# Attention and two dense layers on one core: the four transfers of q of items 8 to 15 issued by ScalarE instead of SyncE

## The chip, the cores and the metric

One Trainium2 chip, one of its cores. The time of a kernel is the device time of one execution in microseconds (us), the median of the runs shown. A profile is one further execution, recorded by the hardware profiler. Engines are called as in the profile: PE is TensorE, PEld its weight loads, DVE is VectorE, ACT is ScalarE, POOL is GpSimd, SP is SyncE, which computes nothing and issues transfers. An engine's name with a q (SPq, ACTq) is its instruction queue: there stand the instructions that issue transfers or wait.

## What is computed

Three steps follow each other. Attention takes q, k and v of shape (4 batches, 8 heads, 576 positions, 64). Then come two dense layers over the 2304 x 512 result: a maximum of three products followed by an output product, and a product of two products followed by an output product.

```python
q_d, k_d, v_d = (x.reshape(B, H, S // 4, 4, D).mean(axis=3) for x in (q, k, v))
out_up = np.repeat(sm_attn(q_d, k_d, v_d), 4, axis=2)
scores = np.where(np.abs(pos[:, None] - pos[None, :]) < 4, scale * q @ k.T, -1e9)
out_local = softmax(scores) @ v
x = (out_up + out_local).transpose(0, 2, 1, 3).reshape(2304, 512)
h = np.maximum(np.maximum(x @ w1, x @ w2), x @ w3) @ w_out
return ((h @ w_a) * (h @ w_b)) @ moe2_w_out
```

## The kernel before, in words

**Items.** The attention is cut into 16 items, each two heads of one batch. An item goes through these steps: k and q are loaded (`a_load_qk`), v is loaded in two forms (`a_load_v`: vr for the averaged attention, L248, and vw for the local windows, L272), k and q are turned so that the head dimension lies on partitions (`a_qk`), scores and softmax (`a_scores`: exponentials on ACT at L376 and L395, normalisations on POOL at L401 and L408), transposes of the probabilities (`a_tr`: POOL folds four rows of v together at L419 and L420, PE transposes, ACT copies out of PSUM at L435 and L447) and the products with v (`a_av`, L456 and L478, sums on DVE at L488, high and low parts on ACT at L501 and POOL at L502).

**Two ways to turn k and q.** Items 0 to 7 are loaded with rows of 64 numbers and turned by PE (L309, L314). Items 8 to 15 (`i >= TV`) are loaded so that each 32 x 32 block already stands in place: four transfers for k and four for q (L228), each 32 partitions x 576 numbers, 72 KB in pieces of 32 numbers. DVE then turns the blocks (L296 for k, L297 for q).

**Buffers.** The tiles of k, q, vr and vw have one buffer in each pool. Items 8 to 15 alternate between the pools `ap_` (even) and `ex2` (odd); items 0 to 7 alternate between `ap_` (even) and `ex` (odd). So the load of an item waits until the item two before it has been read in the same pool: q for L297 of that item, vr for L420 of that item. The first tile in `ex2` (item 9) has no such wait.

**Order of the work.** Up to the line `ctx.enter_context(tc.manual_schedule())` (L1422) the program's tile framework decides the order of each engine's instructions. It plays the program through a timeline of its own with the priorities that the code gives (the strings LOOP and LOOPS set in which order the steps of different items are written: k is the load of k and q, v the load of v, Q the turning, S, T and A the rest). Work of the first dense layer is mixed in as filler (`dense`, matmuls at L700), and pieces of its weights are loaded at L523 and converted on DVE, ACT and POOL (L544 to L567). An engine then runs its own list strictly in order; an instruction that waits holds everything behind it on that engine. From L1422 on the order is written out by hand, and the change touches nothing there.

**What the change touches.** Line L228 alone. In the kernel before, all transfers of the attention are issued by SP.

Of the kernel before, what the change touches and what calls it, by code (L numbers as in the profile page):

```python
# [64 lines left out]
def attn_moe_kernel(  # L65
# [14 lines left out]
    nc = tc.nc  # L80
# [121 lines left out]
    def pool2(i):  # L202

        return ex2 if i >= NI // 2 and i % 2 else pool(i, 2)
# [12 lines left out]
    def a_load_qk(i):  # L217
        b, hp = items[i]
        s = st[i]
        h = 2 * hp  # L220
        engs = (nc.sync, nc.scalar if i < ACT_LOADS else nc.sync)
        if i >= TV:
            for nm, src in (("k", k), ("q", q)):
                x = pool2(i).tile([P, (RF + 1) * 2 * D], F32, tag=nm, bufs=1, name=nm)
                s[nm] = x[:, :S]
                for j in range(P // BS):
                    hh, d0 = divmod(j * BS, D)
                    nc.sync.dma_start(  # L228
                        x[j * BS : (j + 1) * BS, :S].rearrange("p (c d) -> p c d", d=BS),
                        src[b, h + hh, :, d0 : d0 + BS].rearrange("(c p) d -> p c d", p=BS),  # L230
                    )
            return
        for eng, nm, src in zip(engs, "kq", (k, q)):
            s[nm] = pool2(i).tile([P, RF + 1, 2, D], F32, tag=nm, bufs=1, name=nm)
            for j in range(2):
                eng.dma_start(
                    s[nm][:, :RF, j, :], src[b, h + j, : RF * P].rearrange("(r p) d -> p r d", p=P)
                )
            eng.dma_start(
                s[nm][:RT, RF], src[b, h : h + 2, RF * P :].rearrange("h p d -> p h d")  # L240
            )
# [1146 lines left out]
    def emit(f, i):  # L1388
        if i < NI and (f, i) not in emitted:
            emitted.add((f, i))  # L1390
            {"k": a_load_qk, "v": a_load_v, "Q": a_qk, "S": a_scores, "T": a_tr, "A": a_av}[f](i)
# [283 lines left out]
```

## Time and profile before

| | |
|---|---|
| median of 3 runs | 848.06 us (846.41 to 849.1) |
| the profiled execution's own time | 848.16 us |
| its span, first to last instruction | 846.4 us |
| mean granted TensorE clock | 0.982 |
| PE busy | 818.0 us (97%) |
| DVE, ACT, POOL busy | 650.9, 355.6, 441.0 us |
| attention's transfers of lines L228, L248, L272 | from 57.6 us on for L228, until 182 us for L272 |

The chain that ended last is the path of work, followed back from the last instruction. A timeline row gives start, duration, engine, line, operation, output and inputs, the number of merged instructions, and in brackets how long the engine had been idle before and what ended the wait.

### The profile page before, as it was taken

The page shows a single profiled execution, that of the slowest core. Times are in us where ns is not written, and L with a number is a line of the kernel's source. Part 1 is how long each engine was busy: PE and PEld are TensorE (multiplying, and loading weights), DVE is VectorE, ACT ScalarE, POOL GpSimd, SP SyncE. Part 2 cuts the span into 40 slices and gives each one's busy share as a digit, 9 for nine tenths or more (in the row PEclk, how much of TensorE's full clock was granted, in tenths as well). Part 3 has the DMA queues.
Part 4 walks back from the last instruction along what each step waited for, and adds up shares of the span by engine and source line. Part 5 has one row for each costly group of instructions (what it writes and reads, how often), then busy time and mean ns, then how long its engine had stood idle before and what let it go on. Part 6 is the DMA issues. An engine that isn't in the chain of part 4 may idle for free.

```text
span 846.4 us, 15417 instructions
## 1 busy us (share of the span) xinstructions
PE 818.0 (97%) x5785; PEld 767.2 (91%) x5785; DVE 650.9 (77%) x1220; ACT 355.6 (42%) x812; POOL 441.0 (52%) x417
## 2 busy tenths in 40 slices
PE   5988799999999999999999999999999999999998
PEld 3767589999999999999989999999999999999997
DVE  4896986754989688689689689798888745577775
ACT  4785555544343223324246543444443432333331
POOL 3876586535456335546557645545554543355541
PEclk9699989999999999999999999999999999999999
DMA  7899975200321111320144554454442358766612
GB/s 175 182 191 163 171 124 110 43 21 2 124 75 50 51 50 50 137 75 26 68 156 174 189 189 168 179 187 171 178 174 106 143 207 330 259 225 224 225 51 74
DMA packets 125555, 116.33 MB, mean 137 GB/s; under 512 B 81834, under 2 KB 108202, under 8 KB 125482
## 3 DMA queue, kind: packets, MB, share of 16 engines
q1 hardware_dynamic: 121162, 98.06, 39.9%
q10 hardware_dynamic: 4320, 17.30, 5.7%
q8 instruction: 45, 0.74, 0.4%
q14 instruction: 28, 0.23, 0.1%
HBM read 80.74 MB, written 34.60 MB: 136 GB/s over the span
## 4 chain that ended last, share of the span: by engine, by line
PE 86%; DMA 5%; DVE 3%; POOL 3%; issue 1%; SPq 1%; ACT 1%; POOLq 0%; DVEq 0%; ACTq 0%
PE ps_m L700 40%; PE ps_u L1091 30%; PE ps_q L865 5%; PE ps_m L1241 4%; DMA vr<-in_v_dram 2%; PE ps_av L478 1%; PE ps_tl L441 1%; DMA raw<-in_moe_w_out_dram 1%; PE ps_ud L456 1%; PE ps_s L358 1%; PE ps_sd L340 1%; PE ps_m L865 1%; DMA vw<-in_v_dram 1%; POOL vr L419 1%; PE ps_td L430 1%
## 5 line engine op out<-in xcount | busy, mean ns | idle before, releaser
L700 PE MATMUL ps_m<-xh,w 128*128 128x384 f32 x864 | 173.7, 339 | 0.3 <-ACT xh L501 0.3
L700 PEld LDWEIGHTS ps_m<-xh,w 128*128 128x128 f32 x864 | 151.2, 189 | 1.7 <-ACT xh L501 0.6
L1091 PE MATMUL ps_u<-xh,w 128*128 128x384 f32 x720 | 136.8, 336 | 0.1
L1091 PEld LDWEIGHTS ps_u<-xh,w 128*128 128x128 f32 x720 | 125.3, 188 | 1.9 <-DVE acc L756 0.5
L1091 PE MATMUL ps_u<-xl,w 128*128 128x384 f32 x648 | 122.5, 335 | 0.4 <-ACT sn L1103 0.4
L1091 PEld LDWEIGHTS ps_u<-xl,w 128*128 128x128 f32 x648 | 112.9, 188 | 2.2 <-ACT sn L1103 0.7
L1103 ACT COPY sn<-ps_u 128x384 f32<-128x384 f32 x108 | 51.2, 479 | 123.5 <-PE ps_u L1091 120.3
L1281 POOL TENSOR_TENSOR gl<-g,gh 128x384 fp32r<-128x384 f32 x52 | 54.7, 1053 | 83.3 <-ACT gh L1280 83.3
L700 PE MATMUL ps_m<-xl,w 128*128 128x384 f32 x432 | 94.4, 337 | 0.2 <-POOL xl L502 0.2
L700 PE MATMUL ps_m<-wo,gh 128*128 128x512 f32 (+1 forms) x316 | 92.4, 390 | 0.0
L700 PEld LDWEIGHTS ps_m<-xl,w 128*128 128x128 f32 x432 | 76.5, 188 | 0.9 <-POOL xl L502 0.4
L700 PEld LDWEIGHTS ps_m<-wo,gh 128*128 128x128 f32 x316 | 58.4, 188 | 9.6
L729 DVE TENSOR_TENSOR t<-ps_m,t 128x384 f32<-128x384 f32 x48 | 26.4, 551 | 45.1 <-PE ps_m L700 38.4
L1022 POOL TENSOR_TENSOR w<-F,w 128x768 fp32r<-128x768 f32 (+1 forms) x36 | 56.3, 1578 | 9.2 <-ACT w L1020 8.7
L551 ACT ACTIVATE ce<-ce,ebias 128x512 int16<-128x512 uint16 x60 | 43.4, 723 | 41.0 <-DVE ce L544 41.0
L1350 DVE TENSOR_TENSOR acc<-ps_m,acc 128x512 f32<-128x512 f32 (+1 forms) x67 | 45.0, 677 | 18.7 <-PE ps_m L700 18.4
L554 DVE SCALAR_TENSOR_TENSOR ce<-raw,ce 128x512 uint16<-128x512 uint16 x60 | 49.8, 830 | 3.6 <-ACT ce L551 3.5
L1115 DVE TENSOR_TENSOR ca<-ps_u,sn 128x384 f32<-128x384 f32 x54 | 30.0, 555 | 28.8 <-PE ps_u L1091 17.9
L1033 POOL TENSOR_TENSOR F<-F 128x256 f32<-128x256 f32 x24 | 20.1, 839 | 59.3 <-DVE F L561 49.5
L700 PE MATMUL ps_m<-wo,gl 128*128 128x512 f32 (+1 forms) x158 | 48.9, 391 | 0.0
L1233 DVE TENSOR_TENSOR acc<-ps_m,acc 128x512 f32<-128x512 f32 (+1 forms) x62 | 33.3, 552 | 15.4 <-PE ps_m L1241 13.1
L544 DVE TENSOR_SCALAR ce<-raw 128x512 uint16<-128x512 uint16 x60 | 39.1, 652 | 2.1 <-DMA raw<-in_moe_w_dram 1.7
(209 smaller groups left out, 1684.6 us busy)
## 6 DMA issues: line engine op xcount, KB each, us to landing
dw<-w SPq DMA_DIRECT2D x24, 768.0 KB
raw<-in_moe_w_dram SPq DMA_DIRECT2D x18, 512.0 KB
raw<-in_moe_w_out_dram SPq DMA_DIRECT2D x18, 512.0 KB
w<-dw SPq DMA_DIRECT2D x12, 768.0 KB
w<-dw ACTq DMA_DIRECT2D x12, 768.0 KB
dw<-wo SPq DMA_DIRECT2D x12, 512.0 KB
vw<-in_v_dram SPq DMA_DIRECT2D x62, 80.0 KB
vr<-in_v_dram SPq DMA_DIRECT2D x16, 288.0 KB
```

The lines of the kernel that those rows point to most:

```text
L544: nc.vector.tensor_scalar(out=e, in0=top, scalar1=0x7FF0, scalar2=None, op0=ALU.bitwise_and)
L551: nc.scalar.activation(out=s16, in_=e, func=AF.Relu, bias=ebias, scale=8.0)
L554: nc.vector.scalar_tensor_tensor(out=e, in0=top, scalar=0x8000, in1=e, op0=ALU.bitwise_and, op1=ALU.bitwise_or)
L700: nc.tensor.matmul(ps, lhs[a], rhs[b], start=(i == 0), stop=(i == n - 1))
L865: nc.tensor.matmul(ps, sw[c0, n][a][:, m * P : (m + 1) * P], hq[n][b], start=start and k == 0, stop=k == 2, skip_group_check=not start,)
L1022: nc.gpsimd.tensor_tensor(out=l, in0=w, in1=h.bitcast(F32), op=ALU.subtract)
L1091: nc.tensor.matmul(ps, w[:, a, slot, kk], y[:, b * HK + kk], start=start and i == 0, stop=i == 3 * HK - 1, skip_group_check=not start,)
L1103: nc.scalar.copy(t, ps)
L1233: nc.vector.tensor_tensor(out=a, in0=x, in1=a, op=ALU.add)
L1241: nc.tensor.matmul(y, lhs[a], tw[c, n][b], start=start and k == 0 and t == ts.start, stop=k == 2, skip_group_check=True,)
L1281: nc.gpsimd.tensor_tensor(out=l, in0=g, in1=h.bitcast(F32), op=ALU.subtract)
L1350: nc.vector.tensor_tensor(out=a, in0=ps, in1=a, op=ALU.add)
```

## The change

The four transfers of q of an item from 8 to 15 are issued from ACT's queue. Those of k stay on SP's. Nothing else is edited.

```diff
@@ -225,7 +225,7 @@
                 s[nm] = x[:, :S]
                 for j in range(P // BS):
                     hh, d0 = divmod(j * BS, D)
-                    nc.sync.dma_start(
+                    (nc.scalar if nm == "q" else nc.sync).dma_start(
                         x[j * BS : (j + 1) * BS, :S].rearrange("p (c d) -> p c d", d=BS),
                         src[b, h + hh, :, d0 : d0 + BS].rearrange("(c p) d -> p c d", p=BS),
                     )
```

## Rows read from the trace of the kernel before

**Rows 1.** The page's first part: busy time, share and instructions of each engine

```profile
PE 818.0 (97%) x5785; PEld 767.2 (91%) x5785; DVE 650.9 (77%) x1220; ACT 355.6 (42%) x812; POOL 441.0 (52%) x417
```

**Rows 2.** Busy time by stretch: stretch, us, engines busy, PEclk, DMA share, GB/s

```profile
57.00:70.00 13.00, 12.52 (x206) 9.96 (x208) 11.55 (x35) 9.95 (x31) 9.13 (x12) 1.00 0.94 164
70.00:80.00 10.00, 8.85 (x122) 7.08 (x114) 5.96 (x14) 6.37 (x20) 5.66 (x8) 1.00 0.91 160
80.00:90.00 10.00, 5.18 (x95) 3.95 (x95) 8.82 (x19) 1.90 (x5) 6.24 (x7) 0.95 0.94 161
90.00:100.00 10.00, 9.67 (x130) 7.83 (x127) 9.06 (x21) 6.38 (x20) 7.00 (x7) 0.88 0.93 166
100.00:110.00 10.00, 7.43 (x36) 6.07 (x36) 10.00 (x23) 5.79 (x19) 7.24 (x8) 0.80 1.13 190
110.00:120.00 10.00, 10.00 (x127) 8.37 (x126) 7.80 (x22) 6.84 (x22) 8.25 (x10) 0.86 0.56 117
120.00:130.00 10.00, 10.00 (x100) 9.61 (x99) 7.48 (x21) 4.50 (x12) 7.61 (x9) 1.00 0.73 119
```

**Rows 3.** The chain that ended last, 0 to 110 us: start, us, what

```profile
63.74 4.29 DMA vr<-in_v_dram
...
70.78 5.13 DMA vr<-in_v_dram
...
98.81 3.82 DMA vr<-in_v_dram
```

**Rows 4.** Timeline of SP: the transfers as it issues them

```profile
67.37 3.31 SPq L228 DMA_DIRECT2D q<-in_q_dram  x6
70.78 1.67 SPq L248 DMA_DIRECT2D vr<-in_v_dram  x2
...
95.26 2.06 SPq L228 DMA_DIRECT2D q<-in_q_dram  x4
...
98.81 0.42 SPq L248 DMA_DIRECT2D vr<-in_v_dram  x1
...
132.65 0.31 SPq L248 DMA_DIRECT2D vr<-in_v_dram  x1
```

**Rows 5.** Timeline of POOL

```profile
62.71 0.72 POOL L420 TENSOR_TENSOR vd<-vr 72x256 f32<-72x256 f32 x1
...
76.04 1.27 POOL L419 TENSOR_TENSOR vr<-vr 72x512 f32<-72x512 f32 x1 [3.72 <-DMA vr<-in_v_dram]
...
95.82 0.72 POOL L420 TENSOR_TENSOR vd<-vr 72x256 f32<-72x256 f32 x1
...
102.76 1.86 POOL L419 TENSOR_TENSOR vr<-vr 72x512 f32<-72x512 f32 x1 [3.97 <-DMA vr<-in_v_dram]
...
136.74 1.29 POOL L419 TENSOR_TENSOR vr<-vr 72x512 f32<-72x512 f32 x1 [1.73 <-DMA vr<-in_v_dram]
```

**Rows 6.** Timeline of DVE

```profile
71.66 0.78 DVE L297 STREAM_TRANSPOSE qt<-q 128x576 f32<-128x576 f32 x1 [2.21 <-DMA q<-in_q_dram]
...
81.18 1.11 DVE L547 TENSOR_SCALAR cm<-raw 128x512 uint32<-128x512 uint32 x1 [3.56 <-POOL w L567]
```

**Rows 7.** Timeline of PE

```profile
88.81 0.30 PE L345 MATMUL ps_s<-cap,identb 128*128 128x320 bf16 x1 [3.50 <-DVE el L392]
...
106.04 1.33 PE L441 MATMUL ps_tl<-ident,el 128*128 128x128 f32 x5 [2.45 <-POOL el L408]
```

**Rows 8.** Lines L228 and L1077: engine, operation, count, ns min/median/max, first and last start

```profile
L228 SPq DMA_DIRECT2D q<-in_q_dram x32: 384/496/764, 60.3 to 139.9; - x32
...
L1077 ACTq DMA_DIRECT2D w<-dw x18: 326/326/443, 690.8 to 797.0; - x18
L1077 ACTq DMA_DIRECT2D raw<-dw x6: 326/486/1466, 695.0 to 790.4; - x6
```

**Rows 9.** Timeline of ACT

```profile
73.05 0.63 ACT L566 CAST w<-cm 128x512 fp32r<-128x512 f32 x1 [3.12 <-DVE cm L561]
```

**Rows 10.** Waits of SP's queue, 57 to 120 us: total us, times, longest

```profile
SPq L228 <- DVE sd L398: 1.0, 1, 1.0
```

## Prediction

> **What bounds the kernel now.** I read the page first: PE is busy for 97% of the span [rows 1]. So a change in the attention counts only where PE stands still or runs slowly, and the next view to read is the busy time by stretch. From 120 us on PE has no gap: 10.00 of 10 us at a granted clock of 1.00. The stretch in which the moved transfers start is another matter. From 57 to 120 us PE is busy for 12.52 + 8.85 + 5.18 + 9.67 + 7.43 + 10.00 = 53.65 of 63 us, so it idles for 9.35 us; and from 80 to 120 us its granted clock is 0.95, 0.88, 0.80 and 0.86, which withholds 0.5 + 1.2 + 2.0 + 1.4 = 5.1 us of full-rate time [rows 2]. These 14.5 us are all that can be won. No time saved later than 120 us can count.
>
> The third view is the chain that ended last, as far as 110 us. Transfers of vr stand on it three times, of 4.29, 5.13 and 3.82 us [rows 3]. They are not slow: one issued at 132.65 us, where SP has little to do, releases POOL's addition at 136.74 us, 4.09 us later [rows 4, 5]. They start late. The timeline of SP shows why: ahead of the vr at 70.78 us stand six transfers of q that take 3.31 us to issue, and ahead of the one at 98.81 us four of q, 2.06 us [rows 4]. Their buffers had long been free. The first (item 7) reuses the buffer of item 5, read by the sixth L420, which ends at 62.71 + 0.72 = 63.43 us. The second (item 10) reuses that of item 8, read by the ninth, which ends at 95.82 + 0.72 = 96.54 us [rows 5]. So SP's strict order made these transfers wait for 7.35 and 2.27 us.
>
> What follows from it is in the timelines of POOL, DVE and PE. POOL idles 3.72 us before its addition at 76.04 us and 3.97 us before the one at 102.76 us [rows 5]. Behind the first stands a weight conversion on POOL that DVE awaits for 3.56 us, until 81.18 us; DVE also lost 2.21 us at 71.66 us to q itself [rows 6]. PE pays a little later, 3.50 us before 88.81 us and 2.45 us before 106.04 us [rows 7]. In each case the low clock follows the gap [rows 2].
>
> **The change, part by part.** It removes 32 issues from SP, each with a median of 496 ns, between 60.3 and 139.9 us [rows 8]: 15.9 us of SP's time. Eight of them, those of items 8 and 9, fall before 71 us.
>
> Gain 1, the vr of item 7: without the six q issues it starts 3.3 us earlier. POOL's wait of 3.72 us nearly goes, and DVE's 3.56 us with it. DVE has other work up to then and is busy for 8.82, 9.06 and 10.00 of 10 us afterwards [rows 2], so it is the next to be late. I take 3.0 us; the bounds are 0 (DVE or ACT late instead) and 3.56.
>
> Gain 2, the vr of item 10: it can start at 96.6 instead of 98.81 us, 2.2 us earlier, and POOL's wait falls from 3.97 to about 1.8 us. PE's gap of 2.45 us stands behind that addition by way of POOL's L408, so I take 2.0 us, with bounds of 0 and 2.2.
>
> Gain 3, the clock: the two gaps of PE come before the low-clock stretches. If both shrink below what lowers the clock, up to 5.1 us return; if neither does, nothing. I take 1.0, because gap 1 keeps part of its cause, DVE's load.
>
> The cost is on ACT. The nearest rows for an issue from ACT are 326 ns for a 768 KB transfer and 486 ns for another (longest 1466) [rows 8]; the same pieces cost SP 496 ns, and I take that value. It makes 2.0 us per item and 15.9 us in all, bounded by 32 x 0.326 = 10.4 us and, with one slow issue per item, 8 x (3 x 0.496 + 1.466) = 23.6 us. From 70 to 130 us ACT idles for 60 - 31.8 = 28.2 us [rows 2], against 24 x 0.496 = 11.9 us: covered, if the issues stand in those gaps. An example is the 3.12 us that ACT waits before 73.05 us [rows 9]. From 57 to 70 us it is not covered: ACT idles there for 13 - 9.95 = 3.05 us against 8 x 0.496 = 4.0 us. Behind the issues stand the copies out of PSUM and the exponentials, and PE and DVE wait for these. The earlier q repays part of it, because DVE's wait of 2.21 us [rows 6] becomes shorter. I take a net cost of 2.0 us; the bounds are 0 and 4.0 plus the waits below.
>
> A wait is also moved. From item 10 on a q issue waits until DVE has turned the q two items before it (L297). On SP the longest wait of this line is 1.0 us, once [rows 10]. On ACT such a wait would hold L376, L395, L435 and L447 of older items. Lower bound 0, upper bound 1.0 us for each of the 6 items from 10 on, 6 us; I take 0, as the one long wait is alone among 64 issues. SP's remaining issues only move forward, and no instruction on POOL or DVE is added. After 120 us eight or so of the issues fall where PE has no gap, and I price them at nothing. What hides them is ACT's idle time, 5.5 of 10 us [rows 2]; without it each item would cost up to 2.0 us.
>
> The sum, against the profiled execution (848.16 us, span 846.4, so 1.8 us around it): -3.0 - 2.0 - 1.0 + 2.0 = -4.0, and 848.16 - 4.0 = 844.2. That execution is 0.1 us above the median of 848.06, so 844.1 us against the median.
>
> **The first rival: ACT becomes what SP was; slower.** Place: ACT from 57 to about 110 us, where q's issues stand in front of copies that PE needs. Price: 2.0 us for each of the five items 8 to 12 that are loaded while PE has no reserve, 10 us. The gains are then halved by the late ACT, -2.5, and the clock falls no less often. Result: 848.1 + 7.5 = 855.6 us at worst and about 852 if half of it is covered. It decides when two or more items are issued while ACT has other work ready, or ahead of L297 of the item that frees the buffer. For it speaks ACT's 9.95 of 13 us up to 70 us; against it the 28.2 us of idle time after that [rows 2]. The order on ACT is written by the planner's own timeline, and the trace of before cannot show it; that raises the chance. I give this 0.32.
>
> **The second rival: the transfers themselves are the limit; no change.** The 16 DMA engines are 0.94, 0.91, 0.94 and 0.93 busy from 57 to 100 us [rows 2], and q's share is unchanged by the edit: the same pieces of 128 bytes. A vr issued earlier would share the engines with q and land no earlier: 848.1 us. Against it: vr takes 4.29 and 3.82 us in the crowd [rows 3] and 4.09 us out of it [rows 4, 5], so no queue stands in front of it; and the share reaches 1.13 in one stretch, so 0.93 is not the ceiling [rows 2]. The Trainium skill (DMA: Bandwidth & Descriptors, Issuing engines are not separate DMA queues) speaks against the change here: transfers from SP and ACT run on the same 16 engines and interleave, and a second issuer saves the sequencer's time alone, which it calls usually small relative to the transfer. By that rule the result would be 848.1 us. The trace agrees that the engines are shared, but not that the issue time is small here: six issues take 3.31 us next to a vr of 4 to 5 us [rows 3, 4]. Together with the case in which gains and costs cancel (gains of 3, costs of 3) I give no change 0.20.
>
> **A third: more moves than the diff says.** The planner orders the whole attention anew once q has another queue. Filler and conversions can change places by some us either way. I can price that only as a widening of both sides by 2 us; a better or worse order counts in the chances above.
>
> **How the numbers follow.** Forecast, faster: 0.48; no change 0.20; slower 0.32. The measurement of this kernel can tell about 0.3% from no change, 2.5 us. The forecast's own range reaches from 838.5 (gains 3.56 + 2.2, most of the clock, a cost of 1 us) to 845.5 us. For 8 in 10 the range must take in no change and the half-covered rival: 839.5 to 853.0, which leaves out the worst of the first rival and the best of the forecast.
>
> **What the profile of the changed kernel would show.** SP: 32 q issues fewer, and item 7's vr issued near 67 us. POOL: the waits for vr of 3.72 and 3.97 us shorter by about 3 and 2 us. DVE: no wait of 3.56 us behind POOL's conversion and none of 2.2 us for q. PE: less than 6 us idle from 57 to 120 us. ACT: 32 issues of about 0.5 us. The forecast is wrong if PE's or DVE's waits for ACT (L315, L435, L447, L395) grow by more than 4 us in all, if ACT stands before q issues for L297, or if vr takes 6 us or more from issue to landing while q is under way from ACT.

## The result, and the profile after

The changed kernel is slower: 854.38 us, the median of 4 runs (853.26 to 854.98), against 847.93 us for the kernel before in the same sitting (846.41 to 849.1). The ratio is 1.0073, with a 95% interval of 1.0056 to 1.0091. That is 6.45 us, more than the 0.3% that a measurement can tell, and 1.4 us above the range of the prediction.

The first part of the page of after answers to [rows 1].

```profile
PE 819.0 (96%) x5785; PEld 768.4 (90%) x5785; DVE 656.6 (77%) x1220; ACT 354.7 (42%) x812; POOL 441.1 (52%) x417
```

PE does the same work in a span of 853.2 us, 6.8 us longer. ACT's computing takes 354.7 us; it was 355.6. The 32 transfers that it issues now aren't in this number, because the profile doesn't count issues as busy time.

**Where the time goes** is read from busy time by stretch: from, to, us, then the busy time of PE, PEld, DVE, ACT and POOL with their instructions, the granted clock, the DMA share and GB/s. First the kernel before, for the two longer stretches that [rows 2] don't have:

```profile
0.00:57.00 57.00, 43.17 (x498) 32.74 (x498) 43.30 (x108) 35.15 (x110) 34.91 (x53) 0.82 0.87 184
57.00:120.00 63.00, 53.66 (x691) 43.27 (x691) 53.19 (x131) 37.24 (x114) 43.52 (x49) 0.92 0.91 160
```

Then the kernel after:

```profile
0.00:57.00 57.00, 37.92 (x436) 29.20 (x437) 39.58 (x97) 32.28 (x101) 31.43 (x50) 0.82 0.92 176
57.00:120.00 63.00, 53.70 (x699) 43.18 (x697) 55.77 (x132) 36.37 (x110) 41.27 (x45) 0.92 1.00 158
...
57.00:70.00 13.00, 9.74 (x118) 7.48 (x117) 6.60 (x23) 4.82 (x14) 5.66 (x7) 0.74 1.20 169
...
120.00:150.00 30.00, 29.33 (x354) 26.04 (x350) 23.35 (x54) 15.49 (x45) 21.82 (x25) 1.00 0.68 117
```

PE loses 43.17 - 37.92 = 5.25 us in the first 57 us, in which the kernel before issued none of the moved transfers. From 57 to 120 us, the stretch that the prediction was made of, nothing changes on balance: 53.70 and 53.66 us at the same clock. After 120 us PE now has 0.67 us of gaps. These make 5.9 of the 6.8 us.

A second reading confirms that the loss lies early. L488 is the sum that ends an item's attention; two stand per item. The row of the line gives count, ns, and the first and last start: before, then after.

```profile
L488 DVE TENSOR_TENSOR x<-ps_av,up x32: 407/445/464, 32.2 to 201.0; 128x290 f32<-128x290 f32 x16, 128x286 f32<-128x286 f32 x16
```

```profile
L488 DVE TENSOR_TENSOR x<-ps_av,up x32: 409/444/460, 37.1 to 207.9; 128x290 f32<-128x290 f32 x16, 128x286 f32<-128x286 f32 x16
```

The first sum comes 4.9 us later and the last 6.9 us. Behind the last, 846.4 - 201.0 = 645.4 us were left before and 853.2 - 207.9 = 645.3 us are left after. In the traces of all variants below this rest is 644.9 to 645.6 us. So one number, the start of the last L488, tells of any variant what it cost.

**What else the trace of after shows.** The transfers of L228: on which queue, count, ns min/median/max, first and last start.

```profile
L228 ACTq DMA_DIRECT2D q<-in_q_dram x32: 317/332/668, 0.7 to 148.0; - x32
L228 SPq DMA_DIRECT2D k<-in_k_dram x32: 311/402/1472, 34.5 to 148.5; - x32
L228 ACTq EVENT_SEMAPHORE  x10: 17/28/5022, 56.3 to 144.8; - x10
```

The first q no longer starts at 60.3 us [rows 8] but at 0.7 us. Item 9's tile is the first in its pool and waits for no buffer, so the planner made its four issues the first instructions of ACT. The timelines of ACT and PE show what this does to the first turn (in after; in before PE began the turn of k at 4.38 us and that of q at 6.13 us):

```profile
0.74 2.18 ACTq L228 DMA_DIRECT2D q<-in_q_dram  x4
...
4.99 1.09 PE L309 MATMUL ps_t<-ident,k 128*128 128x128 f32 x4 [4.99 <-DMA k<-in_k_dram]
7.54 1.11 PE L309 MATMUL ps_t<-ident,q 128*128 128x128 f32 x4 [1.47 <-DMA q<-in_q_dram]
```

Later, ACT stands at the first issue of item 8. Timelines of ACT and of DVE in after:

```profile
56.57 0.22 ACT L316 COPY kt<-ps_t 128x64 f32<-128x64 f32 x1
61.55 1.87 ACTq L228 DMA_DIRECT2D q<-in_q_dram  x2
63.53 0.47 ACT L395 ACTIVATE el<-el 128x320 f32<-128x320 f32 x1 [6.74 <-DMA q<-in_q_dram]
...
64.03 0.49 DVE L405 TENSOR_REDUCE eps<-el 128x5 f32<-128x320 f32 x1 [4.45 <-ACT el L395]
```

ACT computes nothing for 6.74 us, its queue waits for 5.02 us at one instruction, and DVE then waits 4.45 us for ACT. The issue does not wait for L297. The kernel's instruction list tells for what: the transfers of SP and ACT take eight completion semaphores in turn, and a transfer waits until the one that had its semaphore before has landed. For ACT's first issue of item 8 the list reads

```
L228 DMA q<-in_q_dram 32x18x32 [waits DMAHW5,DMAHW4,DMAHW6,DMAHW3,DMAHW7,DMAHW1,DMAHW0]
```

that is, for landings on seven of the eight, all of transfers that SP issued. Six of them are earlier loads of q. The seventh, DMAHW4, is the semaphore that this issue takes itself: the transfer that had it before is the first load of k of item 7, which SP issued only at 56.16 us.

Last, the planner wrote another order of the whole attention, for all engines. SP's own loads moved too: in after, SP issues two transfers of k of item 9 ahead of those of k of item 5.

```profile
34.52 0.95 SPq L228 DMA_DIRECT2D k<-in_k_dram  x2
35.58 2.81 SPq L236 DMA_DIRECT2D k<-in_k_dram  x2
```

In before, the first transfer of L228 starts at 57.58 us. So three theories stood: **A**, item 9's early transfers and the new order of the first 57 us; **B**, ACT's time (the first rival); **C**, ACT's waits for landings of SP's transfers.

### The profile page after: what moved, and what is told of

Same layout as the page of the kernel before. It is cut to its first block, busy times and chain, and to the rows that moved or that the text cites. A ratio compares the mean times of both kernels' runs of the same rounds, so it can differ in the third digit from the quotient of the medians.

```text
span 853.2 us, 15403 instructions
## 1 busy us (share of the span) xinstructions
PE 819.0 (96%) x5785; PEld 768.4 (90%) x5785; DVE 656.6 (77%) x1220; ACT 354.7 (42%) x812; POOL 441.1 (52%) x417
## 4 chain that ended last, share of the span: by engine, by line
PE 81%; DMA 7%; DVE 5%; POOL 3%; issue 2%; SPq 1%; ACT 1%; POOLq 0%; DVEq 0%; ACTq 0%
PE ps_m L700 37%; PE ps_u L1091 30%; PE ps_q L865 4%; PE ps_m L1241 4%; DMA vr<-in_v_dram 4%; DMA q<-in_q_dram 1%; DMA raw<-in_moe_w_out_dram 1%; PE ps_m L865 1%; POOL xl L502 1%; PE ps_s L358 1%; PE ps_av L478 1%; PE ps_sd L340 1%; DMA k<-in_k_dram 1%; PE ps_ud L456 1%; POOL el L408 1%
## 5 line engine op out<-in xcount | busy, mean ns | idle before, releaser
L544 DVE TENSOR_SCALAR ce<-raw 128x512 uint16<-128x512 uint16 x60 | 42.9, 716 | 4.5 <-DMA raw<-in_moe_w_out_dram 3.9
```

The costliest lines, as they stand in the source:

```text
L544: nc.vector.tensor_scalar(out=e, in0=top, scalar1=0x7FF0, scalar2=None, op0=ALU.bitwise_and)
```

## The experiments

The ratios are to the kernel before, measured in the same sitting. Executions of the kernel before ranged from 844.48 to 851.44 us in one sitting (29 runs), so verdicts rest on the ratios, and a trace is read only for where a wait stands.

### Which items' transfers carry the loss

Each of these replaces the condition at L228 and leaves the planner free.

```diff
-(nc.scalar if nm == "q" else nc.sync).dma_start(
+(nc.scalar if nm == "q" and i == 9 else nc.sync).dma_start(    # e1
+(nc.scalar if nm == "q" and i == 8 else nc.sync).dma_start(    # e2
+(nc.scalar if nm == "q" and i != 9 else nc.sync).dma_start(    # e3, e9
```

Item 9 alone (e1). 

> Only the four q transfers of item 9 go to ACT; all others stay on SP. Theory A (the early issue): nothing holds item 9's q back, so the planner puts it first on ACT, the first loads of items 0 and 1 come later and the order of the first 57 us is another; most of the loss is there. It expects 851 to 854 us against 848, PE's first turn of q near 7.5 us instead of 6.1, and PE busy for some 38 of the first 57 us as in the changed kernel. Theory B (ACT's time: 2 us per item that is moved, the first rival): one item of eight, so 0.9 us at most, 848 to 849 us. Theory C (ACT waits for landings of SP's transfers, worst at item 8): no loss here, 848 us.

Measured: 855.62 us, ratio 1.0087 (1.0057 to 1.0117), above even A's range. Four issues in place of 32 give the whole loss, and the last of them starts at 2.4 us, so ACT spends no time on q later. B falls.

Item 8 alone (e2). 

> Only the four q transfers of item 8 go to ACT. Theory C: ACT stands about 5 us near 56 us, before the first of them, until transfers that SP issued have landed, and this costs 2 to 5 us: 850 to 853 us. Theory A: no early issue, 848 us, give or take what the new order costs. Theory B: 0.9 us at most, 848 to 849 us.

Measured: 848.17 us, 1.0005 (0.9987 to 1.0024): no difference. ACT's longest wait for a landing is 1.7 us here, so this is no test of C.

All but item 9 (e3). 

> As the changed kernel, but item 9's q stays on SP: seven items on ACT. Theory A: the loss at the start is undone, PE's first turn of q is back near 6.1 us and the time is 847 to 850 us. Theory B: seven eighths of the loss remain, 853 to 854 us. Theory C: ACT's wait of about 5 us near 56 us remains, 850 to 853 us.

Measured: 844.67 us, 0.9961 (0.9945 to 0.9977). It beats both kernels, which no theory had expected, although ACT stands 4.5 us at item 8's issue.

### Taking the early issue away

The `with` lines are cut behind the condition: what follows is the issue, from ACT for all q in e4 and for item 9's q in e6 and e7.

```diff
+with tc.issue_after(mark["q", i - 2].ins) if nm == "q" else ExitStack():                # e4
+with tc.issue_after(mark["q", 0].ins) if nm == "q" and i == 9 else ExitStack():         # e6
+with tc.issue_after(mark["q", 7].ins) if nm == "q" and i == 9 else ExitStack():         # e7
+(nc.scalar if nm == "q" and i >= 10 else nc.sync).dma_start(                            # e5
+(nc.scalar if i >= 10 else nc.sync).dma_start(                                          # e8, k and q
```

All q on ACT, each held behind L283 of the item two before (e4). 

> As the changed kernel, but the planner is told to queue each item's q transfers on ACT behind the scaling of q of the item two before (the L283 that follows the turn that frees the buffer). No early issue, and ACT's order up to 57 us is that of the kernel before. Theory A: the loss at the start is gone, 845 to 849 us, and the gains on POOL's waits for vr may show. Theory B: all eight items still cost ACT their 2 us, 853 to 855 us. Theory C: the 5 us wait near 56 us shrinks to under 2 us because the issue stands later, but waits of 1 to 2 us at other items remain, 848 to 852 us.

Measured: 854.26 us, 1.0082 (1.0059 to 1.0105). A's expectation missed: without an early issue the kernel is as slow. C's missed too: ACT stands 6.8 us at one issue, not under 2.

Items 10 to 15 (e5). 

> Items 10 to 15 issue q from ACT, items 8 and 9 from SP. If ACT's stand of 3 to 6 us before item 8's first issue is a cost (it waits there for landings of transfers that SP has just issued), leaving it out beats the kernel with seven items on ACT (844.7 us): 839 to 843 us. If that stand was covered anyway, 844 to 846 us. If the gain of the seven-item kernel came from the two first items leaving SP (the vr of item 7 behind six issues of q), it is lost here: 847 to 849 us.

Measured: 851.03 us, 1.0042 (1.0029 to 1.0054), outside all three ranges.

Item 9 alone, held behind item 0's turn (e6). 

> Only item 9 on ACT, its issue queued behind the scaling of q of item 0 (about 10.5 us instead of 0.7). The first turn of item 0 is no longer in competition with it. If the loss of 8 us is the direct delay of the first loads (PE's first turn of q 1.4 us late, and what follows from it), this gives 847 to 850 us. If it is the order that the planner writes once item 9's early transfers stand among the loads of items 1 to 4, most of it stays: 852 to 856 us.

Measured: 853.08 us, 1.0074 (1.006 to 1.0089). The issues come at 7.8 us, out of the way of the first turn, and the loss stays.

Item 9 alone, behind item 7's turn (e7). 

> Only item 9 on ACT, its issue queued behind the scaling of q of item 7 (about 63 us), where SP had it. Both forms of the early-issue theory expect the time of the kernel before within 2 us: 846 to 850 us. If a single item on ACT costs by ACT's time or by waits for landings, 849 to 852 us.

Measured: 850.95 us, 1.0046 (1.0029 to 1.0063), in the range of the waits and of ACT's time.

k and q of items 10 to 15 (e8). 

> Items 10 to 15 issue q and k from ACT: 48 issues. An issue from ACT runs beside ACT's computing in the profiles so far, so that ACT's time does not grow, and SP loses 24 more issues ahead of vr and vw: as the six-item kernel or 1 to 2 us better, 838 to 845 us. If ACT's time counts (the rival of the prediction), 12 us more of issue on ACT cost 3 to 6 us: 847 to 852 us.

Measured: 849.37 us, 1.0027 (1.0016 to 1.0038), in the second range; whether by ACT's time or by the long stand that the next rows show is open.

In e5, e7 and e8 ACT stands once for very long at an issue. The waits of ACT in these three (total us, times, longest):

```profile
ACT w L566 <- DMA vw<-in_v_dram: 8.9, 1, 8.9
```

```profile
ACT ptd L435 <- DMA vw<-in_v_dram: 6.2, 1, 6.2
```

```profile
ACT up L465 <- DMA vw<-in_v_dram: 9.4, 1, 9.4
```

In e1 and e6 nothing of this kind happens, and they lose more than these three (0.87% and 0.74%). So C can't be the whole either. What all slow kernels share, with e2 and e3, is that the planner wrote another order. Of nine newly planned orders (after, e1 to e8) seven are slower than before, one is level, one is faster.

### The order and the issuer taken apart

These kernels are planned twice. The first pass records the order of the attention that the planner writes with q of the items in REC on ACT. The second puts q of the items in RUN on ACT and keeps the recorded order of every engine by edges between neighbours; only the moved issues are left out of the chain, and may be placed behind L283 of a given item. PE, DVE, ACT and POOL then run the recorded list instruction by instruction, and SP issues its other transfers in the recorded order. Lines of L228 carry a helper's line number here, L1661.

```diff
+    for n in state["order"]:                  # the order of the first pass
+        x = traced[n]
+        if x.name in moved:
+            continue
+        if x.engine in last:
+            tc.add_manual_dep(x, last[x.engine].name, no, reason="pin_order")
+        last[x.engine] = x
```

```diff
+REC, RUN, PLACE = set(), set(), {}                                # p6: order of before, all q on SP
+REC, RUN, PLACE = {8..15}, set(), {}                              # p1: order of after, all q on SP
+REC, RUN, PLACE = {8,10..15}, set(), {}                           # p2: order of e3, all q on SP
+REC, RUN, PLACE = set(), {8..15}, {i: i - 2}                      # p3: order of before, all q on ACT
+REC, RUN, PLACE = set(), {9}, {}                                  # p4: order of before, item 9 first on ACT
+REC, RUN, PLACE = set(), {9..15}, {i: i - 2 for i > 9}            # p5: item 8 on SP, 9 first
+REC, RUN, PLACE = set(), {9..15}, {i: i - 1 for i > 9}            # p7: as p5, issued one item later
```

The control (p6). 

> Control: the kernel before with its own order on every engine kept by fixed edges, all q on SP. 846 to 849 us; any difference from the kernel before is what the edges themselves cost.

Measured: 848.04 us, 1.0004 (0.9988 to 1.002). The edges cost nothing that the runs can tell.

The changed order without the change (p1). 

> The changed kernel's order on PE, DVE, ACT and POOL, instruction by instruction, is kept by fixed edges, but all 32 issues of q go back to SP, none ahead of the others' place in its queue. The theory of the order (the planner's new sequence is what costs): it stays slow, 852 to 856 us, as the changed kernel. The theory of the issuer (q on ACT costs, by early transfers, by ACT's time or by ACT's waits for landings): 846 to 849 us, as the kernel before.

Measured: 855.26 us, 1.0085 (1.0067 to 1.0103). No q is issued by ACT, and the kernel is as slow as the changed one. The loss is the order's, that of SP's other loads included; engines and SP were not taken apart. One place where it arises is seen on PE. First the kernel before (start, us, engine, line, operation):

```profile
27.00 1.33 PE L441 MATMUL ps_tl<-ident,el 128*128 128x128 f32 x5 [0.57 <-POOL el L408]
28.28 1.09 PE L309 MATMUL ps_t<-ident,k 128*128 128x128 f32 x4
29.29 1.23 PE L456 MATMUL ps_ud<-ptd,vd 72*64 72x144 f32 x8
30.45 1.59 PE L478 MATMUL ps_av<-pt,vw 64*64 64x58 f32 x40
```

Then p1:

```profile
28.87 1.09 PE L309 MATMUL ps_t<-ident,k 128*128 128x128 f32 x4 [4.00 <-DMA k<-in_k_dram]
29.75 1.27 PE L441 MATMUL ps_tl<-ident,el 128*128 128x128 f32 x5
30.96 1.23 PE L456 MATMUL ps_ud<-ptd,vd 72*64 72x144 f32 x8
...
36.26 1.35 PE L478 MATMUL ps_av<-pt,vw 64*64 64x58 f32 x38
```

In the new order the turn of a later item's k stands ahead of the first finished item's L441, waits 4.00 us for its load, and holds that item's transposes; the products L478 were put behind the turn and the scores of other items, most of them 5.8 us later. The first L488 starts at 37.7 us in p1, the last at 208.3.

The faster order without the change (p2). 

> The order of PE, DVE, ACT and POOL of the 844.67 us kernel (all q on ACT but item 9's), kept by fixed edges, with all q issued by SP. The theory of the order: 843 to 846 us, the gain stays without any issue on ACT. The theory of the issuer (SP relieved, vr earlier): the gain goes, 847 to 850 us.

Measured: 845.67 us, 0.9977 (0.9963 to 0.9991). A gain with no issue on ACT at all; of e3's gain of 0.39% the order alone holds 0.23%, and the intervals overlap.

Item 9 early, in the order of before (p4). 

> The kernel before's order on PE, DVE, ACT and POOL, kept by fixed edges; only item 9's four issues of q on ACT, as its first instructions. The theory of early transfers (they delay the first loads): 851 to 856 us, as with item 9 alone (855.62). The theory of the order: 846 to 850 us, the 0.4 to 1.4 us that the first turns are late and no more.

Measured: 846.48 us, 0.9984 (0.9971 to 0.9997). The early transfers cost no time in the end. They do delay the first turn as in after, and PE's first 57 us; in the next stretch, where PE was short of work anyway, most of it comes back:

```profile
0.00:57.00 57.00, 39.79 (x451) 30.49 (x452) 42.43 (x103) 33.82 (x105) 34.14 (x51) 0.85 0.95 183
57.00:120.00 63.00, 56.46 (x747) 45.99 (x746) 56.70 (x138) 39.06 (x120) 46.62 (x52) 0.92 0.92 161
```

The move alone (p3): what the prediction's sum priced. 

> The kernel before's order on PE, DVE, ACT and POOL, kept by fixed edges; all 32 issues of q on ACT, each held behind the end of the turn (L283) of the item two before it. This is what the prediction priced: the move alone. The prediction's sum: 843 to 846 us. The first rival (ACT's time and its waits): 850 us or more. The theory of the order says only that it is nearer to 848 than the changed kernel is: 844 to 850 us.

Measured: 848.57 us, 1.0008 (0.9991 to 1.0025): no change. On ACT the wait is there again, at item 8's first issue:

```profile
61.91 0.95 ACTq L1661 DMA_DIRECT2D q<-in_q_dram  x2
62.96 0.39 ACT L435 COPY ptd<-ps_td 72x288 f32<-72x288 f32 x1 [6.20 <-DMA k<-in_k_dram]
```

A second one of 5.0 us follows at an L726, and PE waits 4.1 and 3.9 us for L435. The trace is that of p3's slowest execution (852.39 us).

### In which stretch, and where the predicted gain went

The order of before up to L283 of item 7 (about 57 us), then a free planner with all q on ACT (h1); and the order of after up to the same point, then a free planner with all q on SP (h2).

```diff
+        if rest:                              # only behind the kept part, otherwise free
+            if x.name not in moved and x.engine in last:
+                tc.add_manual_dep(x, last[x.engine].name, no, reason="pin_order")
+            continue
+        rest = x.name == mark["q", 7].ins.name
```

> All q on ACT, item 9's first, as in the changed kernel; but up to the end of item 7's turn (L283, about 57 us) each engine keeps the kernel before's order by fixed edges, and the planner is free only after that. If the loss lies in the planner's new order of the first 57 us (PE busy 37.92 us there, 43.17 before): 845 to 850 us. If it lies in what follows (item 8's wait on ACT, the later order): 852 to 856 us.

Measured: 851.55 us, 1.005 (1.0032 to 1.0069), between the two expectations. ACT's longest wait for a landing from 57 to 150 us is 2.5 us.

> All q on SP, as in the kernel before; but up to the end of item 7's turn each engine keeps the changed kernel's order, and the planner is free after that. If the loss lies in the first 57 us: 851 to 856 us without a single issue on ACT. If it lies later: 845 to 849 us.

Measured: 854.9 us, 1.0089 (1.006 to 1.0118). Busy time by stretch, first h1, then h2:

```profile
120.00:150.00 30.00, 27.32 (x349) 23.67 (x347) 23.05 (x50) 15.21 (x42) 21.01 (x25) 1.00 0.61 100
```

```profile
0.00:57.00 57.00, 38.28 (x435) 29.77 (x435) 40.06 (x96) 32.22 (x101) 32.11 (x50) 0.76 0.84 174
57.00:120.00 63.00, 53.44 (x699) 43.44 (x700) 58.20 (x135) 37.09 (x111) 40.28 (x45) 0.92 0.92 158
```

In h2's trace PE loses 4.89 us by 57 us and 0.22 us from there to 120 us, with q on SP: the changed order of the first 57 us is enough for the loss there. But h1's newly planned rest costs too, with 2.68 us less of PE from 120 to 150 us than the 30.00 us of before. The two don't add up to the loss of after, so it can't be put down to one place in the order.

Item 8 left on SP (p5). 

> The kernel before's order on PE, DVE, ACT and POOL kept; q of items 9 to 15 on ACT (9's first, the others held behind L283 of the item two before), item 8's left on SP, so that ACT need not stand 6.2 us behind item 8's first issue. If that wait is what ate the prediction's gains in the 848.57 us kernel: 842 to 846 us, POOL's waits for vr near 76 and 103 us shorter. If the gains were never there, or the later waits of ACT (5.0 us at L726 there) weigh as much: 847 to 850 us.

Measured: 848.52 us, 1.0017 (1.0002 to 1.0032). The first gain that was predicted is in the trace, and so is what eats it. POOL, ACT and PE in p5:

```profile
72.99 1.29 POOL L419 TENSOR_TENSOR vr<-vr 72x512 f32<-72x512 f32 x1
...
80.02 3.19 ACTq L1661 DMA_DIRECT2D q<-in_q_dram  x4
83.25 0.48 ACT L726 COPY t<-ps_m 128x384 f32<-128x384 f32 x1 [8.45 <-DMA vr<-in_v_dram]
...
85.48 1.23 PE L456 MATMUL ps_ud<-ptd,vd 72*64 72x144 f32 x8 [8.66 <-ACT ptd L435]
```

The row at 72.99 us is item 7's addition. POOL no longer waits for its vr, where it waited 3.72 us [rows 5]. A profile is one execution, though, and the control p6 has 1.74 us at this place (items 7 and 9 in one row):

```profile
73.49 2.94 POOL L419 TENSOR_TENSOR vr<-vr 72x512 f32<-72x512 f32 x2 [1.74 <-DMA vr<-in_v_dram]
```

Then ACT stands 8.45 us behind item 10's first issue, and PE 8.66 us for a copy behind it.

The same, issued one item later (p7). 

> As p5_before_not8 (order of before kept, item 8's q on SP, 9's first on ACT), but q of items 10 to 15 stands on ACT behind L283 of the item before it, about 12 us later, when the transfers whose completion semaphores it takes over should have landed. If ACT's stand behind item 10's first issue (8.45 us there) ate the gain: no such wait over 2 us, and 842 to 846.5 us. If the gain of the earlier vr is lost to something else (the clock, DVE): 846.5 to 850 us.

Measured: 845.47 us, 0.9975 (0.9958 to 0.9991). Only the place of 24 issues differs from p5, and the intervals don't meet. POOL and ACT in p7:

```profile
73.42 1.29 POOL L419 TENSOR_TENSOR vr<-vr 72x512 f32<-72x512 f32 x1 [0.34 <-DMA vr<-in_v_dram]
...
87.46 0.32 ACTq L1661 DMA_DIRECT2D q<-in_q_dram  x1
87.82 0.35 ACT L501 CAST xh<-x 128x192 fp32r<-128x192 f32 x1
...
93.43 0.90 POOL L420 TENSOR_TENSOR vd<-vr 72x256 f32<-72x256 f32 x1 [1.00 <-PE ps_ud L456]
...
100.95 1.27 POOL L419 TENSOR_TENSOR vr<-vr 72x512 f32<-72x512 f32 x1 [1.48 <-DMA vr<-in_v_dram]
```

Its busy time from 57 to 120 us, then that of the control p6:

```profile
57.00:120.00 63.00, 57.13 (x758) 46.91 (x752) 60.47 (x135) 38.75 (x118) 46.63 (x50) 0.92 0.86 152
```

```profile
57.00:120.00 63.00, 55.80 (x724) 46.08 (x720) 57.90 (x136) 38.84 (x117) 45.20 (x50) 0.95 0.89 158
```

ACT's longest wait for a landing is 1.2 us, and POOL's waits at both places are shorter than in before. PE is busy for 57.13 us of the stretch in place of 53.66, but the control, with nothing moved, has 55.80 us in its profiled execution (843.98 us, the fastest of its twelve). So the gain rests on the ratios and not on this row. C is a price of its own, beside the order: with the order the same, p5 and p7 differ by 0.42%. That it is the shared semaphores and not another wait for a landing rests on the instruction list; semaphores of ACT's own were not tried.

The best version again (e9, the kernel of e3). 

> The kernel of e3_q9sp (all q on ACT but item 9's, the planner free), measured again with more rounds as the version that beat both: 843 to 846 us, 0.2 to 0.5% under the kernel before.

Measured: 843.75 us, 0.9954 (0.9934 to 0.9973).

## Why the prediction was wrong, point by point

**The bound: right.** All of the difference arises before the last L488; 645 us behind it are the same to 0.1 us.

**The failed step: the third rival, "more moves than the diff says".** The prediction let every issue stay where SP had it, and priced the new order as "a widening of both sides by 2 us". The order alone is worth 0.85% (p1), about 7 us, the whole of the result, and between the best and the worst newly planned order (e3 and e1) lie 11 us. No row of the trace of before could have told the sign. But that q of item 9 waits for no buffer, and so would go to the front of a queue that has nothing else to issue, could be read from the code.

**Gain 1: the mechanism right, its worth open.** With the order kept, POOL's wait of 3.72 us for item 7's vr is gone in p5 and 0.34 us in p7; in the control it is 1.74 us. **Gain 2: not shown.** In p7 POOL's wait for item 10's vr falls from 3.97 to 1.48 us, but the vr doesn't start sooner after its buffer is free. SP in p7:

```profile
88.92 7.13 SPq L1661 DMA_DIRECT2D k<-in_k_dram  x3
96.15 0.55 SPq L248 DMA_DIRECT2D vr<-in_v_dram  x1
```

The buffer is free at 93.43 + 0.90 = 94.33 us, so the vr still starts 1.82 us late, now behind issues of k; the prediction had read 2.27 us, and the control, with q on SP, has 1.22 us. Item 10's addition starts at 100.95 us in p7 and at 101.00 us in the control. **Gain 3**, the clock, is not seen where it was forecast: 0.92 from 57 to 120 us in before, after and p7, 0.95 in the control. Over all executions p7's mean granted clock is 0.986, that of before in the same sitting 0.983, so a part of p7's gain may be the clock's; the runs don't separate it. The sum of -4.0 was too large: the best that the move brought in the order of before is 2.1 us (p7), of which p4's four early issues alone make 0.9 us; the two intervals overlap.

**The cost on ACT: mis-sized.** 0.496 us per issue, 15.9 us in all, were taken from SP's row. On ACT the median is 0.332 us in after and 0.318 to 0.542 us in the variants, and an issue lies beside ACT's computing (last section). No run shows the 2.0 us of net cost in this form.

**The moved wait, priced at nothing, is the second failure.** The prediction looked at the wait for a buffer (L297) alone, with an upper bound of 6 us in all. What came is a wait for landings: 6.74 us in after, 6.2 and 5.0 us in p3, 8.45 us in p5. With the order kept it stands between p5, without a gain, and p7, with one.

**The first rival** gave 852 to 855.6 us and so the number, by luck and not by its cause: with all q on ACT in the old order (p3) nothing is lost. **The second rival**, no change, is what p3 shows; the rule of the Trainium skill (DMA: Bandwidth & Descriptors, Issuing engines are not separate DMA queues) would give 848.1 us there, and the 848.57 us agree. Not for its reason alone, though: p3's ACT stands 6.2 and 5.0 us, and p7, where it doesn't, is 0.25% faster than before. That this is the time of SP's queue is argued, not shown.

**What was to show it wrong** did in part. PE's and DVE's waits for the four lines of ACT grow from 1.3 to 5.8 us from 57 to 120 us, 4.45 us of it DVE's one wait for L395. ACT stands before q issues, though not for L297. Item 9's vr, issued at 68.16 us, let POOL's addition start at 74.26 us, 6.1 us later and just over the 6 us named. PE idles 9.3 us in that stretch, not under 6.

## What to carry to other kernels

Where a planner writes the order, an edit of one queue is two changes: keep the old order with edges to price the edit, and keep the edit out to price the order. An issue moved onto a computing engine cost little here by its own time; what it cost is what it waited for, so place it where the transfers that had its completion semaphore before have landed. And a transfer that waits for no buffer goes to the front of an idle queue unless it is held.

## What the runs showed of the hardware

An issue on ACT's queue runs beside ACT's computing. Timeline of ACT in after: the copy at 78.20 us lasts until 78.60, and an issue starts and runs within and past it.

```profile
78.20 0.40 ACT L435 COPY ptd<-ps_td 72x288 f32<-72x288 f32 x1 [2.02 <-DMA vw<-in_v_dram]
78.28 0.37 ACTq L228 DMA_DIRECT2D q<-in_q_dram  x1
78.49 0.47 ACT L395 ACTIVATE el<-el 128x320 f32<-128x320 f32 x1
```

The wait ahead of an issue doesn't run beside it: it holds all later work of the engine, for up to 9.4 us (e8). The same 72 KB in pieces of 128 bytes took a median of 332 ns to issue from ACT in after, and 402 ns from SP, which had 496 ns in before [rows 8]. That relieving SP makes its issues shorter is not shown: in p3, with all q on ACT, SP's k has 498 ns.
